# A recurrent-memory transformer with a planned instruction order: 64-column values in place while one layer runs, and seven early groups staged over the GpSimd DMA queue

## The chip, the cores and the metric

The kernel runs on one core of one Trainium2 chip. The metric is device time in microseconds (us), from the first to the last instruction of one execution. Before the change it is 1634.84 us, the median of three runs from 1634.42 to 1636.5 us. In the profile PE is TensorE (PEld is its weight load), DVE is VectorE, ACT is ScalarE, POOL is GpSimd and SP is SyncE. DMAs are issued from SP, ACT and POOL.

## The reference, cut to what matters

Two layers, each an attention over segments and a dense block, are applied to x of 2048 x 512. The attention is recurrent: 8 memory rows that come out of segment s go into segment s + 1.

```python
for s in range(n_seg):                       # 64 segments of 32 rows
    h = concat([mem, xs])                    # 8 + 32 = 40 rows
    q, k, v = h @ Wq, h @ Wk, h @ Wv         # 32 heads of 128
    p = softmax(where(mask, q @ k.T * scale, -1e9))
    o = (p @ v) @ Wo
    mem = o[:8]; outs.append(o[8:])
# x = x + A(layernorm(x));  x = x + relu(layernorm(x) @ w1) @ w2;  and both once more
```

## The kernel before, in words

**Steps.** The kernel walks through 68 steps. In step k, layer 0 works on segment k and layer 1 on segment k - 4 (`DELTA = 4`). So steps 0 to 3 have layer 0 alone with 40 columns, steps 4 to 63 have both layers side by side in 80 columns, and steps 64 to 67 have layer 1 alone. A step projects queries and keys for 32 heads (L1074), scores (L1103), runs the softmax on DVE and ACT (L1114 to L1145), turns the probabilities (L646), multiplies them with the values (L1187) and projects with Wo (L1214). The new memory columns are copied from PSUM into the next step's input tile `HT` by DVE (L1230). That copy ends one step and starts the next. After every second step a "dense unit" (`finish_pair`, `dense_layer`) does the dense block of two segments; its hidden tile is `hT`.

**Values.** The value rows of x do not depend on the recurrence. They are computed ahead by groups of four segments. Groups 0 to 5 (`EARLY = 5`) are *early*: `prepare_group` loads the rows, `layernorm` normalises and turns them, and `early_values` computes four 64-column units of eight matmuls each (L973) while the weights are still arriving. Groups 6 to 15 are *late*: pairs of groups are made in the steps by `late_values` (L944), eight units of four 128-column matmuls per pair. All late values and those of groups 1 to 5 are written to HBM (`vh`) and come back by DMA into the value tile `V0` as needed. Only the columns that hold the rest of a segment and its memory rows are computed in the step, with 32 columns (`values_narrow`, L992) in steps 1 to 3 and with 64 columns from step 4; they get from the tile `vw` into `V0` by DMA (L1026). Step 0 computes 40 columns straight into `V0` (`values_direct`, L1038). Group 0's rows wait in the tile `vg` (L1014).

**Where early data waits.** The rows of x land in two halves of `vw`. The values of groups 1 to 5 wait in the room of the weights `w1` and `w2` until POOL's queue has written them to HBM (L932). Their normalised rows wait in tiles `xg`. SP writes those to HBM (`xh`, L811) once the marker "loaded" says that step 1's values have been placed. The dense weights are loaded after that.

**Weights.** Wv (in three parts), Wq, Wk and Wo (in halves) are loaded at the start. All but the first part go over POOL's queue, and their order there is Wv, Wv, Wq, Wk, Wq, Wk, Wo, Wo (L498, L495).

**Order.** Every operation is put into a plan with a cost, what it reads and what it writes. `Plan.order` lists them by planned start, with priorities from the tables `PLACE` and `AHEAD` and four numbers in `RULE`. The program is written in that order, and each engine executes its instructions strictly in it. A DMA is modelled by `bulk` as an issue on the engine and a landing on a serial queue. The plan charges a matmul order that changes the column tiling (`tile`) with `TURN`.

A layernorm crosses four engines: DVE (L684, L687), POOL for the power of -1/2 (L690, L691), DVE for the scaling (L694), PE for the turn (L646), then ACT or DVE for the copy (L894, L896).

Of the kernel before, what the change touches and what calls it, by code (L numbers as in the profile page):

```python
# [26 lines left out]
WHOLE, COL64, EITHER, COL32 = range(4)  # L27
TURN = 0.096

RULE = (0.0731, 331.4491, 505.4188, 866559925356557.625)  # L30
PERIOD = 46.2777
PLACE = {
    ("attend.mmu0.0", 0): -152.667, ("attend.mmu0.0", 1): -118.912, ("attend.mmu0.0", 2): -639.225,
    ("attend.mmu0.0", 3): 328.193, ("attend.mmu0.0", 4): -173.499, ("attend.mmu0.0", 5): 386.967,
    ("attend.mmu0.0", 6): 449.133, ("attend.mmu1.0", 0): -183.38, ("attend.mmu1.0", 1): 433.744,
    ("attend.mmu1.0", 2): 361.711, ("attend.mmu1.0", 3): 441.403, ("attend.mmu1.0", 4): -122.568,
    ("attend.mmu1.0", 5): 199.077, ("attend.mmu1.0", 6): 581.404, ("attend.mmu2.0", 0): -862.741,
    ("attend.mmu2.0", 1): -762.821, ("attend.mmu2.0", 2): -99.412, ("attend.mmu2.0", 3): -218.396,
    ("attend.mmu2.0", 4): -720.778, ("attend.mmu2.0", 5): -60.014, ("attend.mmu2.0", 6): -142.579,
    ("attend.mmu3.0", 0): -166.299, ("attend.mmu3.0", 1): -129.893, ("attend.mmu3.0", 2): -1226.967,  # L40
    ("attend.mmu3.0", 3): 67.821, ("attend.mmu3.0", 4): -136.693, ("attend.mmu3.0", 5): -20.817,
    ("attend.mmu3.0", 6): 293.466, ("attend.mmu4.0", 0): 65.898, ("attend.mmu4.0", 1): -215.881,
    ("attend.mmu4.0", 2): 381.601, ("attend.mmu4.0", 3): 412.604, ("attend.mmu4.0", 4): -130.21,
    ("attend.mmu4.0", 5): -853.627, ("attend.mmu4.0", 6): 948.075, ("dense_layer.mm.0", 1): 732.94,
    ("dense_layer.mm.0", 3): 740.199, ("dense_layer.mm.0", 6): 839.326, ("dense_layer.mm.1", 1): -969.556,
    ("dense_layer.mm.1", 3): -286.677, ("dense_layer.mm.1", 6): 67.604, ("dense_layer.mm.2", 1): 398.19,
    ("dense_layer.mm.2", 3): 243.499, ("dense_layer.mm.2", 6): 419.477, ("dense_layer.mm.3", 1): 627.889,
    ("dense_layer.mm.3", 3): 181.496, ("dense_layer.mm.3", 6): 643.035, ("dense_layer.mm.4", 1): 161.37,
    ("dense_layer.mm.4", 3): 390.622, ("dense_layer.mm.4", 6): 400.054, ("dense_layer.mm.5", 1): 594.567,
    ("dense_layer.mm.5", 3): 753.248, ("dense_layer.mm.5", 6): 345.325, ("finish_pair.turn.0", 1): -144.39,  # L50
    ("finish_pair.turn.0", 3): -761.751, ("finish_pair.turn.0", 6): -878.802, ("g0", 2): -907.97,
    ("g1", 2): 259.128, ("g2", 2): -170.342, ("g3", 2): -266.685, ("g4", 2): -99.976, ("g5", 2): 565.774,
    ("late_values.mmv0.0", 0): 283.731, ("late_values.mmv1.0", 0): -248.92, ("late_values.mmv2.0", 0): -1018.714,
    ("late_values.mmv3.0", 0): 469.169, ("late_values.mmv4.0", 0): -1001.105, ("late_values.mmv5.0", 0): 1.489,
    ("late_values.mmv6.0", 0): -868.467, ("late_values.mmv7.0", 0): 433.155, ("layernorm.turn.0", 1): 337.759,
    ("layernorm.turn.0", 3): 441.922, ("layernorm.turn.0", 6): -292.588, ("layernorm.turn.1", 1): -863.663,
    ("layernorm.turn.1", 3): -167.818, ("layernorm.turnr.0", 0): -153.966, ("layernorm.turnr.0", 4): 426.349,
    ("layernorm.turnr.1", 0): 374.651, ("layernorm.turnr.1", 4): 594.017, ("prepare.turns.0", 2): -916.093,
    ("project.mm.0", 0): 352.884, ("project.mm.0", 1): 403.52, ("project.mm.0", 2): 426.265,
    ("project.mm.0", 3): 475.549, ("project.mm.0", 4): -8.363, ("project.mm.0", 5): 481.308,  # L60
    ("project.mm.0", 6): 364.213, ("project.mm.1", 0): 360.97, ("project.mm.1", 1): 250.905,
    ("project.mm.1", 2): 395.025, ("project.mm.1", 3): 90.611, ("project.mm.1", 4): -154.497,
    ("project.mm.1", 5): 342.487, ("project.mm.1", 6): -140.762, ("project.mm.2", 0): 69.475,
    ("project.mm.2", 1): 427.61, ("project.mm.2", 2): -910.526, ("project.mm.2", 3): 539.171,
    ("project.mm.2", 4): -962.774, ("project.mm.2", 5): 327.765, ("project.mm.2", 6): 570.292,
    ("project.mm.3", 0): 234.432, ("project.mm.3", 1): 212.581, ("project.mm.3", 2): 219.168,
    ("project.mm.3", 3): 1057.658, ("project.mm.3", 4): 374.948, ("project.mm.3", 5): 458.206,
    ("project.mm.3", 6): 1049.752, ("project.mm.4", 0): -906.842, ("project.mm.4", 1): -226.675,
    ("project.mm.4", 2): -119.077, ("project.mm.4", 3): 366.414, ("project.mm.4", 4): -955.316,
    ("project.mm.4", 5): 408.222, ("project.mm.4", 6): -222.974, ("queries_keys.mmu0.0", 0): -319.479,  # L70
    ("queries_keys.mmu0.0", 1): -311.142, ("queries_keys.mmu0.0", 2): -195.441,
    ("queries_keys.mmu0.0", 3): -783.942, ("queries_keys.mmu0.0", 4): -856.389,
    ("queries_keys.mmu0.0", 5): -1226.512, ("queries_keys.mmu0.0", 6): -189.749,
    ("queries_keys.mmu0.1", 0): -126.555, ("queries_keys.mmu0.1", 1): -875.245,
    ("queries_keys.mmu0.1", 2): -230.758, ("queries_keys.mmu0.1", 3): -218.806, ("queries_keys.mmu0.1", 4): -924.83,
    ("queries_keys.mmu0.1", 5): -998.214, ("queries_keys.mmu0.1", 6): -798.535, ("queries_keys.mmu0.2", 0): 1.933,
    ("queries_keys.mmu0.2", 1): -915.221, ("queries_keys.mmu0.2", 2): -763.206,
    ("queries_keys.mmu0.2", 3): -815.004, ("queries_keys.mmu0.2", 4): -155.478,
    ("queries_keys.mmu0.2", 5): -920.249, ("queries_keys.mmu0.2", 6): -766.935, ("queries_keys.mmu0.3", 0): -285.59,
    ("queries_keys.mmu0.3", 1): -134.747, ("queries_keys.mmu0.3", 2): 7.492, ("queries_keys.mmu0.3", 3): -23.601,  # L80
    ("queries_keys.mmu0.3", 4): -292.473, ("queries_keys.mmu0.3", 5): -193.042,
    ("queries_keys.mmu0.3", 6): -173.541, ("queries_keys.mmu1.0", 0): -40.306,
    ("queries_keys.mmu1.0", 1): -1010.704, ("queries_keys.mmu1.0", 2): -94.937,
    ("queries_keys.mmu1.0", 3): -233.672, ("queries_keys.mmu1.0", 4): -212.713,
    ("queries_keys.mmu1.0", 5): -961.418, ("queries_keys.mmu1.0", 6): -321.925,
    ("queries_keys.mmu1.1", 0): -965.925, ("queries_keys.mmu1.1", 1): -223.66, ("queries_keys.mmu1.1", 2): -323.504,
    ("queries_keys.mmu1.1", 3): 20.112, ("queries_keys.mmu1.1", 4): -146.653, ("queries_keys.mmu1.1", 5): -223.193,
    ("queries_keys.mmu1.1", 6): -158.937, ("queries_keys.mmu1.2", 0): -823.694,
    ("queries_keys.mmu1.2", 1): -932.252, ("queries_keys.mmu1.2", 2): -231.6, ("queries_keys.mmu1.2", 3): -250.634,
    ("queries_keys.mmu1.2", 4): 237.43, ("queries_keys.mmu1.2", 5): -250.953, ("queries_keys.mmu1.2", 6): -993.941,  # L90
    ("queries_keys.mmu1.3", 0): -189.715, ("queries_keys.mmu1.3", 1): -231.672,
    ("queries_keys.mmu1.3", 2): -257.674, ("queries_keys.mmu1.3", 3): -300.812,
    ("queries_keys.mmu1.3", 4): -145.268, ("queries_keys.mmu1.3", 5): -37.546, ("queries_keys.mmu1.3", 6): -183.014,
    ("queries_keys.mmu2.0", 0): 140.663, ("queries_keys.mmu2.0", 1): -210.356, ("queries_keys.mmu2.0", 2): -294.536,
    ("queries_keys.mmu2.0", 3): -112.732, ("queries_keys.mmu2.0", 4): 320.259, ("queries_keys.mmu2.0", 5): 215.543,
    ("queries_keys.mmu2.0", 6): -122.288, ("queries_keys.mmu2.1", 0): 428.309, ("queries_keys.mmu2.1", 1): 92.511,
    ("queries_keys.mmu2.1", 2): -899.997, ("queries_keys.mmu2.1", 3): 229.222, ("queries_keys.mmu2.1", 4): 280.866,
    ("queries_keys.mmu2.1", 5): 161.233, ("queries_keys.mmu2.1", 6): 27.508, ("queries_keys.mmu2.2", 0): 204.746,
# [82 lines left out]
    ("values_direct.ev", 1): -11.513, ("values_narrow.ev", 1): -7.969,  # L181
}

LOAD = {("v", 0): 4.4, ("v", 1): 3.8, "o": 2.95}
REST, SLOW = 2.75, 6.0

EARLY, SPREAD = 5, (0, 0, 2, 4, 4, 6, 8, 8)


def t_mm(n):  # L190
    return max(0.025, 0.0025 + n / 2400)


# [211 lines left out]
def kernel(  # L405
# [242 lines left out]
    class Early:  # L648

        def __init__(self, g):  # L650
            self.first, self.key = g % 2 == 1, ("xn", g)
            if self.first:
                hold[0] = p_x.buf()
# [698 lines left out]
```

## Time and profile before

| what | value |
|---|---|
| median of three runs | 1634.84 us |
| span of the profile | 1632.0 us |
| busy: PE, DVE, ACT, POOL | 97%, 68%, 64%, 9% |
| ends of steps 0, 1, 2, 3 (start of L1230, from the span's start) | 52.65, 70.62, 89.86, 106.84 us |
| late value matmuls (L944), by the program | 160 |
| 32-column value matmuls (L992) | 96 |
| early 64-column value matmuls (L973 on `xg` and `xnA`) | 160 + 32 |

A line of the timeline gives the start, the time, the engine, the line of the kernel, the operation, the tiles and, in brackets, the idle time of the engine before it with the work that ended it. In the slices, a digit is the busy share of a fortieth of the span in tenths.

### The profile page before, as it was taken

What the parts mean: (1) busy time and instruction counts of PE and PEld (TensorE: products, weight loads), DVE (VectorE), ACT (ScalarE), POOL (GpSimd) and SP (SyncE); (2) the same over time, 40 slices, a digit from 0 to 9 for tenths busy, and PEclk for the clock granted to TensorE, in tenths of its full rate; (3) what the DMA queues carried; (4) which work ended last, traced back from release to release, by engine and by line L of the source; (5) the groups of instructions that cost most, each with busy time, mean ns of one, the idle gap of its engine ahead of it and who ended that gap; (6) DMA issues with size and microseconds to landing.
All of it is one profiled execution on the core that took longest, in us unless ns stands there. A gap on an engine that the chain in (4) does not pass through costs nothing.

```text
span 1632.0 us, 88442 instructions
## 1 busy us (share of the span) xinstructions
PE 1589.6 (97%) x39898; PEld 1377.3 (84%) x39992; DVE 1111.6 (68%) x3091; ACT 1052.5 (64%) x2655; POOL 140.1 (9%) x352
## 2 busy tenths in 40 slices
PE   7999999999999999999999999999999999999997
PEld 4788888888888888888888888888888888888886
DVE  4566776776676676677667667667667767766765
ACT  5566666676666666666667666666666666666664
POOL 3100000000000100000100000100000000000000
PEclk9999999999999999999999999999999999999999
DMA  9720101110110110110110111110110100000000
GB/s 369 231 51 21 27 22 27 41 28 22 28 24 22 41 26 22 25 34 19 38 29 22 28 25 28 35 28 20 28 28 22 26 21 22 19 18 18 18 6 6
DMA packets 47097, 63.89 MB, mean 39 GB/s; under 512 B 17784, under 2 KB 33440, under 8 KB 46720
## 3 DMA queue, kind: packets, MB, share of 16 engines
q1 hardware_dynamic: 41136, 39.09, 10.0%
q0 software_dynamic: 4704, 18.35, 2.9%
q8 instruction: 313, 5.13, 1.4%
q10 hardware_dynamic: 880, 0.80, 0.2%
q14 instruction: 64, 0.52, 0.1%
HBM read 33.50 MB, written 11.93 MB: 28 GB/s over the span
## 4 chain that ended last, share of the span: by engine, by line
PE 92%; DMA 3%; DVE 2%; ACT 2%; issue 1%; POOL 0%; ACTq 0%; SPq 0%; POOLq 0%; DVEq 0%
PE work L1074 37%; PE st L1214 18%; PE fill L973 14%; PE fill L646 10%; PE work L1187 4%; PE work L1103 4%; DMA Wo_sb<-in_A_Wo_dram 2%; PE work L646 2%; PE fill L944 2%; ACT OT L894 1%; DVE HT L1230 0%; PE fill L992 0%; DMA vw<-in_A_x_dram 0%; ACT es L1125 0%; ACT PT L1168 0%
## 5 line engine op out<-in xcount | busy, mean ns | idle before, releaser
L1074 PE MATMUL work<-HT,Wk_sb 128*128 128x80 bf16 (+1 forms) x8704 | 355.7, 199 | 9.6 <-DVE HT L1230 8.8
L1074 PE MATMUL work<-HT,Wq_sb 128*128 128x80 bf16 (+1 forms) x8704 | 349.3, 199 | 1.3 <-DVE HT L1230 0.9
L1214 PE MATMUL st<-OT,Wo_sb 128*128 128x80 bf16 (+1 forms) x8704 | 344.5, 199 | 4.5 <-ACT OT L894 2.5
L1214 PEld LDWEIGHTS <-Wo_sb 128*128 128x128 bf16 x8704 | 324.9, 99 | 28.0 <-issue 5.2
L1074 PEld LDWEIGHTS <-Wq_sb 128*128 128x128 bf16 x8704 | 320.4, 99 | 26.4 <-issue 15.1
L1074 PEld LDWEIGHTS <-Wk_sb 128*128 128x128 bf16 x8704 | 321.6, 99 | 16.4 <-DVE HT L1230 13.3
L894 ACT CAST qT<-work 128x320 bf16<-128x320 f32 (+1 forms) x534 | 219.5, 412 | 76.8 <-PE work L1074 32.4
L973 PE MATMUL fill<-Wv_sb,HT 128*64 128x512 bf16 x2048 | 265.9, 381 | 0.0
L894 ACT CAST kT<-work 128x320 bf16<-128x320 f32 (+1 forms) x510 | 209.9, 412 | 82.5 <-PE work L1074 49.1
L894 ACT CAST OT<-work 128x320 bf16<-128x320 f32 (+1 forms) x404 | 158.1, 417 | 119.8 <-PE work L1187 117.3
L1168 ACT ACTIVATE PT<-work,half 128x320 bf16<-128x320 f32 (+2 forms) x384 | 170.9, 468 | 67.1 <-PE work L646 47.0
L894 ACT CAST vw<-fill 128x512 bf16<-128x512 f32 x203 | 119.0, 586 | 92.5 <-PE fill L973 82.0
L1114 DVE TENSOR_TENSOR es<-work,maskb 128x320 f32<-128x320 f32 (+2 forms) x340 | 136.8, 404 | 45.2 <-PE work L1103 40.3
L1170 DVE TENSOR_SCALAR PT<-work,half 128x160 bf16<-128x160 f32 (+2 forms) x296 | 127.5, 454 | 25.1 <-PE work L646 23.4
L973 PEld LDWEIGHTS <-HT 128*64 128x64 bf16 x2048 | 99.0, 110 | 52.1
L1125 ACT ACTIVATE es<-es 128x320 f32<-128x320 f32 (+2 forms) x340 | 137.6, 410 | 6.0 <-DVE es L1121 5.0
L1121 DVE TENSOR_TENSOR es<-es,mx 128x320 f32<-128x320 f32 (+2 forms) x340 | 136.7, 405 | 5.5
L1118 DVE TENSOR_REDUCE mx<-es 128x8 f32<-128x320 f32 (+2 forms) x340 | 135.2, 400 | 6.2
L1145 DVE TENSOR_TENSOR P<-es,sm 128x320 bf16<-128x320 f32 (+2 forms) x340 | 133.1, 408 | 5.3
L1230 DVE CAST HT<-st 128x64 bf16<-128x64 f32 (+1 forms) x67 | 14.8, 221 | 175.2 <-PE st L1214 175.2
L1128 DVE TENSOR_REDUCE sm<-es 128x8 f32<-128x320 f32 (+2 forms) x340 | 131.6, 396 | 2.5 <-ACT es L1125 1.6
L1103 PEld LDWEIGHTS <-qT 128*40 128x40 bf16 x4096 | 90.8, 98 | 44.8 <-ACT kT L894 10.2
(98 smaller groups left out, 1779.3 us busy)
## 6 DMA issues: line engine op xcount, KB each, us to landing
V<-vw SPq DMA_DIRECT2D x252, 48.0 KB
V<-vh SPq DMA_DIRECT2D x120, 64.0 KB
vh<-vg SPq DMA_DIRECT2D x40, 128.0 KB
Wq_sb<-in_A_Wq_dram POOLq DMA_DIRECT2D x2, 2048.0 KB, 21.3
Wk_sb<-in_A_Wk_dram POOLq DMA_DIRECT2D x2, 2048.0 KB, 25.8
Wo_sb<-in_A_Wo_dram POOLq DMA_DIRECT2D x2, 2048.0 KB, 36.7
Wv_sb<-in_A_Wv_dram POOLq DMA_DIRECT2D x1, 2048.0 KB, 11.8
vh<-w_sb POOLq DMA_DIRECT2D x4, 512.0 KB, 9.9
```

The source lines that it names most:

```text
L646: nc.tensor.matmul(out_[u:v, :], lhsT=lhsT[:, u:v], rhs=rhs, start=start, stop=stop, tile_position=(0, u))
L894: nc.scalar.copy(out=out_, in_=in_)
L973: nc.tensor.matmul(vp[64 * b:64 * b + 64, :], lhsT=cols(c4), rhs=Wv_sb[:, c4, n * 512:(n + 1) * 512], start=(c4 == 0), stop=(c4 == NC4 - 1 ...
L1074: nc.tensor.matmul(qp[:, hi * 2 * L:hi * 2 * L + n], lhsT=W_sb[:, c4, h * Dh:(h + 1) * Dh], rhs=HT[:, c4, c0:c1], start=(c4 == 0), stop=(c ...
L1103: nc.tensor.matmul(v[64 * g2:64 * g2 + L, a, i, b, :], lhsT=qT[:, hi, a * L:(a + 1) * L], rhs=kT[:, hi, a * L:(a + 1) * L], start=True, st ...
L1114: nc.vector.tensor_tensor(out=flat(es[:, A]), in0=flat(sp[:, A]), op=ALU.add, in1=maskb[:, a_lo:a_hi, :].unsqueeze(2).to_broadcast([128, n ...
L1118: nc.vector.tensor_reduce(out=mx[:, As], in_=es3(), axis=AX.X, op=ALU.max)
L1121: nc.vector.tensor_tensor(out=es3(), in0=es3(), op=ALU.subtract, in1=mx[:, As].unsqueeze(2).to_broadcast([128, ns * na, L]))
L1125: nc.scalar.activation(out=es[:, A], in_=es[:, A], func=ACTF.Exp, scale=SCALE)
L1145: (nc.gpsimd if eng == POOL else nc.vector).tensor_tensor(out=o, in0=flat(es[:, A]), op=ALU.mult, in1=sm[:, As].rearrange("p (a s) -> p a ...
L1168: nc.scalar.activation(out=o, in_=i, func=ACTF.Copy, scale=half[:, b:b + 1])
L1214: nc.tensor.matmul(wo[:, 2 * W * c4 + c0:2 * W * c4 + c1], lhsT=Wo_sb[:, h, c4 * 128:(c4 + 1) * 128], rhs=OT[:, h, c0:c1], start=(h == 0 a ...
```

## The change

The change does five things.

1. *One layer only: 64 columns in place.* In steps 0 to 3, `values` computes columns 0 to 63 of `HT` (the 32 rows of the segment, the memory and columns of the other layer) and evicts them whole into `V0`. `values_direct`, `values_narrow` and the column tiling by 32 are gone, and with them the DMAs that place values in steps 1 to 3 and group 0's early values in `vg`.
2. *Seven early groups.* `EARLY` is 7. Groups 6 and 7 are computed with the other early groups, and their values wait in `vg` and `vw`, which nothing else needs yet.
3. *Rows in dense-unit tiles.* The rows of x of the early groups land in two parts of `hT`. Group 7's normalised rows wait in an `OX` tile.
4. *Staging over POOL.* The normalised rows of early groups go to HBM over POOL's DMA queue (`bulk(POOL, ...)`) as soon as they exist, no longer over SP after the marker "loaded".
5. *A new plan.* Late groups start at step 6 and every 12 steps, spread by (0, 0, 2, 4, 4, 6, 8, 10). `RULE`, `PERIOD`, `PLACE` and `AHEAD` have new numbers, so the order changes everywhere.

```diff
-WHOLE, COL64, EITHER, COL32 = range(4)
+WHOLE, COL64, EITHER = range(3)
-EARLY, SPREAD = 5, (0, 0, 2, 4, 4, 6, 8, 8)
+EARLY, SPREAD = 7, (0, 0, 2, 4, 4, 6, 8, 10)
...
-    p_xv = Pool([vw[:, 2 + i, :] for i in range(2)], True)
+    p_xv = Pool([p_h.tiles[0][:, 4 * i:4 * i + 4, :].rearrange("p f t -> p (f t)") for i in range(2)], True)
...
+        if g > 5:
+            return (vg, vw)[g - 6][:, p0:p0 + n, :]
...
-                hold[0] = p_x.buf()
+                hold[0] = (p_x if g < 7 else p_ox).buf()
...
+        if early:
+            def put():
+                nc.gpsimd.dma_start(out=out_, in_=halves_of(xnT))
+
+            bulk(POOL, 0.78, put, ("xh", g), 0.125, w=[("xh", g)], uses=on(xnT))
+            early_values(g, xnT)
...
     def step_values(k):
-        if k == 0:
-            values_direct(HTs[0][:, :, 0:L], deps)
-            return
-        if 1 in act:
-            values(lambda c4: HTs[i][:, c4, HS:2 * L], lambda p: vw[:, p, :], ("vw",), deps)
+        if k < DELTA:
+            values(lambda c4: HTs[i][:, c4, 0:64], lambda p: V0[:, p, :], lambda p: [("V0", p, b) for b in range(2)], deps)
         else:
-            values_narrow(HTs[i][:, :, HS:HS + 32], deps)
-        place_values(k, False)
+            values(lambda c4: HTs[i][:, c4, HS:2 * L], lambda p: vw[:, p, :], lambda p: [("vw", p)], deps)
+            place_values(k, False)
...
-    start = {g: DELTA + 10 * i for i, g in enumerate(pairs)}
+    start = {g: DELTA + 2 + 12 * i for i, g in enumerate(pairs)}
...
-        if k == 1:
-            for put in later:
-                put("loaded")
```

## Prediction

> **What bounds the kernel now.** I read the page's slices first, then the chain of waits, then the timeline of the start by engine.
>
> ```profile
> PE 1589.6 (97%) x39898; PEld 1377.3 (84%) x39992; DVE 1111.6 (68%) x3091; ACT 1052.5 (64%) x2655; POOL 140.1 (9%) x352
> ...
> PE   7999999999999999999999999999999999999997
> PEclk9999999999999999999999999999999999999999
> DMA  9720101110110110110110111110110100000000
> ```
>
> PE is full in all slices but the first and last, and the DMA engines are full only in the first. So there are two stages: a start that ends when the weights have landed, and then a stream of PE work. The chain in order of time shows the seam:
>
> ```profile
> 11.99 38.80 DMA Wo_sb<-in_A_Wo_dram
> 50.83 1.80 PE st L1214 x64
> 54.15 3.07 PE fill L992 x28
> ```
>
> The second half of Wo lands at 11.99 + 38.80 = 50.79 us; then only 64 matmuls of step 0 are left, and step 0 ends at 52.65 (L1230). What else PE does until 50.8 is nearly free; what is queued behind 50.8 is paid in full. The landings follow from the views by line: Wq 21.8, Wk 28.2, Wq 33.6, Wk 38.7 and Wo 45.0 us. POOL in the same stretch:
>
> ```profile
> 28.55 0.22 POOL L690 TENSOR_SCALAR ln<-ln 128x1 f32<-128x1 f32 x1 [6.13 <-DVE ln L687]
> 28.85 0.57 POOL L691 TENSOR_TENSOR ln<-ln,mhalf 128x1 f32<-128x1 f32 x1
> ...
> 43.09 1.20 POOL L932 DMA_DIRECT2D vh<-w_sb  x2 [13.66 <-ACT es L1125]
> 44.46 0.29 POOL L913 COPY HT<-xnA 128x128 bf16<-128x128 bf16 x1 [0.17 <-PE work L1074]
> 44.70 1.06 POOL L932 DMA_DIRECT2D vh<-w_sb  x2
> ```
>
> All layernorm powers of early groups (L690, L691) are done by 29.4, *before* the first staging DMA. That DMA then holds POOL idle for 13.66 us, and nobody needs POOL meanwhile.
>
> ```profile
> DMA to landing us min/median/max: 8.6/9.8/10.9
> ```
>
> This is the view of line L932. Put in at 43.1, behind Wo in the same queue, the first staged values land at 52.1, just after Wo's 50.8: the queue keeps its order.
>
> **What the Trainium skill says.** "DMA: Bandwidth & Descriptors", section "Anatomy of one DMA", says that DMA engines do not wait on semaphores; a wait is held by the issuing sequencer before dispatch. The 13.66 us of idle POOL agree. The same page, "Two DMAs through the same engine are not ordered", says that descriptors of one queue start in order; the landing at 52.1 behind 50.8 agrees. "TensorE: Matmul & The Clock Gate", Part 1, says that an idle window of about 3.4 us halves PE's clock until a busy one has passed; the granted clock is 0.50 between 54 and 56 us, after the wait for Wo, and 28 matmuls of L992 take 3.07 us there, against 16 in about 1.05 elsewhere.
>
> **The change, part by part.**
>
> *Staging over POOL.* The order of the changed program tells the decisive thing. POOL's DMAs use eight completion semaphores in turn, and each issue first waits for the DMA eight places earlier. The eight weight loads take the first turn. Then POOL's program goes on, each item strictly after the one before: rows of group 1 (waits for Wv), powers of groups 2 and 3, values of group 1 and rows of group 2 (wait for Wv and Wq), power of group 4, values of 2 and rows of 3 (wait for Wk and the second Wq, 33.6), power of group 5, values of 3 and rows of 4 (wait for the second Wk, and for the *first half of Wo*, 45.0), power of group 6, values of 4 and rows of 5 (wait for the *second half of Wo*, 50.8, and for group 1's rows, which lie behind it), power of group 7. Before, there were no powers behind such waits.
>
> Queued behind these powers: DVE's scaling of that group stands in DVE's order ahead of the softmax of step 0, and PE's turn of group 6 stands ahead of the second halves of Wq and Wk, that of group 7 ahead of the last keys and of eight value units. So PE stops three times.
> - Group 5: power after 33.6, so its turn is at about 35.5, while PE has run out at about 30. PE then has 6 to 7 us of values; this stop is only partly paid.
> - Group 6: 45.0 + issue 0.55 + power 0.87 (28.55 to 29.42) + scaling 0.41 + 0.1 = 47.0. Then 96 projections of 40 columns, 2.5 us at 25 ns each (64 of L1074 take 1.67 us of weight loads), and PE is empty at about 50.
> - Group 7: one more load of 128 KB beside the weights delays Wo by 0.3, so 51.1 + two issues at 0.55 + 0.87 + 0.41 + 0.1 = 53.6.
>
> Behind group 7's turn still stand, all on PE: the turn 0.4, 32 projections 0.8, the wait for its copy 0.4, eight value units (four of group 7, four of group 6) at 0.866 (eight matmuls of L973) 6.9, scores, turns, attends and changes of tiling about 1.5, and all 128 matmuls of Wo 3.4 (64 took 1.80 with their end). That is 13.4. The idle time before it halves the clock for some 3 us (+1.3). Step 0 ends at 53.6 + 13.4 + 1.3 = 68.3 instead of 52.65: **+15.6 us**. I bound it by 12.5 (no slow clock, waits inside filled) and 18.
>
> *64 columns in place.* A step's values were 32 matmuls of 32 columns, four abreast, 2 x 0.866 = 1.73; they become four units, 3.46: +5.2 over steps 1 to 3. Two units of early groups are left over for step 1: +1.7. Late values and turns of the first late pair leave steps 2 and 3: -2.1. The slow clock of step 1 has moved: -1.4. The placing DMAs (3.7 us of issues on SP after `vw` is ready, but PE waited only 0.4 us for V) give -0.5. Sum **+2.9** (+1 to +5). Group 0's early values (-3.46) are in step 0's sum.
>
> *Fewer late values.* 160 matmuls of L944 become 128. Their price is read from step lengths, from one L1230 to the next in DVE's timeline:
>
> ```profile
> 153.86 0.23 DVE L1230 CAST HT<-st 128x64 bf16<-128x64 f32 x1 [2.18 <-PE st L1214]
> 179.22 0.23 DVE L1230 CAST HT<-st 128x64 bf16<-128x64 f32 x1 [3.31 <-PE st L1214]
> 202.24 0.22 DVE L1230 CAST HT<-st 128x64 bf16<-128x64 f32 x1 [2.73 <-PE st L1214]
> 227.60 0.23 DVE L1230 CAST HT<-st 128x64 bf16<-128x64 f32 x1 [3.30 <-PE st L1214]
> ```
>
> These are steps 6, 7 and 8: 25.36, 23.02 and 25.36 us. An odd step without late values is 22.09 us (1336.77 to 1358.85), with one unit 22.47 (227.60 to 250.07), with two 23.01, for part of a unit fills PE's waits for the softmax. Before: 14 steps of two, 10 of one, from step 4 on, 14 x 0.92 + 10 x 0.38 = 16.7; after, by the program's order: 8 and 16, 13.4. So -3.3, and not the full 8 units x 0.866 = -6.9. One late pair fewer to normalise: -0.3.
>
> *The new order of the 60 double steps.* Step by step PE has the same work and as many changes of tiling (4 and 6 in even and odd steps). More dense matmuls go in 64-column halves (in the timeline 32 halves take 1.02 us, 64 ns a pair, and 16 whole ones 0.90, 56 each), which the steps with that form before show as at most 0.1 us: +1.4. The turns of groups 8 and 9 fall into step 4: +0.5. Waits of DVE and ACT inside a step can move by 0.15 us a pair either way, +-5 us in all. Sum with the late values: **-1.7**.
>
> *At nothing:* the tiles of `hT` and `OX` are free until the first dense unit in step 2, 20 us after; the dense weights wait for staged values that land near 60 us and are first used in step 2; `vg` and `vw` are needed from step 4. PE's work of steps 1 and 2 hides all of it.
>
> Sum: 1634.8 + 15.6 + 2.9 - 1.7 = 1651.6 us.
>
> **The rivals.**
> - *The start is hidden* (6%). If the waits of POOL's issues were met early, groups 6 and 7 would fill PE's idle time before 50.8 (3.7 us from 10 us on), step 0 would end at about 54, and the late values would come off. 1634.8 + 1.3 + 2.9 - 6.9 = 1632 us. It is what the change is for. Against it speaks that each wait stands ahead of a power on the same engine, and that landings are bound by DMA at 400 GB/s.
> - *The same with the saving small* (4%): 1634.8 + 1.3 + 2.9 - 1.7 - 2 = 1635 us.
> - *The start costs, but the stream gains* (20%). If late values save their whole 6.9 and the new order loses a little less in waits, 1634.8 + 13 + 1 - 6.9 = 1642.
> - *Start and stream both lose* (20%). Slow clock twice, and 0.2 us in each of 30 pairs: 1651.6 + 2 + 6 = 1660.
>
> **How the numbers follow.** The likeliest, at 50%, is the stall with an unchanged stream, 1651.6. The range reaches to the 1642 and 1660 cases. Faster 0.06, same 0.04, slower 0.90.
>
> **What would show it.** Right: POOL lines of the new row DMAs with idle time just before 45 to 46 and 51 to 52 us, ended by the weights' DMA; L695 at about 45.6 and 52.2; PE idle 3 to 5 us before the turns that follow; the first memory copy (L1182) near 68 us, the next three about 19, 20 and 18 us apart; then pairs of steps near 48 us. Wrong: the first copy near 54, which would mean that POOL never waited for Wo; or pairs of steps that differ by more than 0.2 us from before, which would put the cause into the stream.

## The result, and the profile after

The kernel after the change takes 1645.74 us (median of four runs, 1644.46 to 1647.37), against 1634.88 before (the three runs above and a fourth); the ratio is 1.0065, with a 95% interval of 1.0048 to 1.0083. It is slower, as forecast, by 10.9 us instead of 16.8. The two profiled executions differ by more, 1645.7 against 1632.0 us: that of after is the slowest of its four runs, that of before is 0.7 us faster than the fastest of its four. So the parts below add up to 13.7, and they are those of single executions.

The page of the kernel after, the lines that answer to those shown of before:

```profile
PE 1600.5 (97%) x40154; PEld 1374.4 (84%) x40154; DVE 1097.8 (67%) x3096; ACT 1056.8 (64%) x2622; POOL 158.0 (10%) x387
...
PE   6899999999999999999999999999999999999998
...
PEclk9899999999999999999999999999999999999999
DMA  9521101101110110111011111101111000000000
```

What is new stands in the first slices: PE is less full in the first two, its clock is lower in the second, and the DMA engines have less to do there. The memory copies that end the steps (DVE's timeline of after) give the sizes:

```profile
67.38 0.19 DVE L1182 CAST HT<-st 128x32 bf16<-128x32 f32 x1 [3.40 <-PE st L1166]
84.39 0.19 DVE L1182 CAST HT<-st 128x32 bf16<-128x32 f32 x1 [1.35 <-PE st L1166]
107.37 0.19 DVE L1182 CAST HT<-st 128x32 bf16<-128x32 f32 x1 [2.09 <-PE st L1166]
123.31 0.19 DVE L1182 CAST HT<-st 128x32 bf16<-128x32 f32 x1 [0.48 <-PE st L1166]
```

| part | before | after | difference | forecast |
|---|---|---|---|---|
| step 0 ends at | 52.65 | 67.38 | +14.7 | +15.6 |
| steps 1, 2, 3 | 17.97, 19.24, 16.98 | 17.02, 22.98, 15.94 | +1.7 | +2.9 |
| steps 4 to 66 | 1495.45 | 1492.99 | -2.5 | -1.7 |
| from there to the end | 29.7 | 29.4 | -0.3 | 0 |

POOL's timeline of after shows the forecast chain, to within half a us:

```profile
33.58 0.55 POOL L817 DMA_DIRECT2D xh<-xg  x1 [4.87 <-DMA Wq_sb<-in_A_Wq_dram]
34.15 0.24 POOL L695 TENSOR_SCALAR ln<-ln 128x1 f32<-128x1 f32 x1
...
45.41 0.55 POOL L817 DMA_DIRECT2D xh<-xg  x1 [5.78 <-DMA Wo_sb<-in_A_Wo_dram]
45.99 0.24 POOL L695 TENSOR_SCALAR ln<-ln 128x1 f32<-128x1 f32 x1
...
51.42 0.62 POOL L937 DMA_DIRECT2D vh<-w_sb  x1 [4.54 <-ACT kT L900]
52.04 0.55 POOL L817 DMA_DIRECT2D xh<-xg  x1
52.61 0.24 POOL L695 TENSOR_SCALAR ln<-ln 128x1 f32<-128x1 f32 x1
```

The three L695 shown are the powers of groups 5, 6 and 7. Each has no idle time of its own (no bracket): it starts the moment the DMA issue before it is through, and that issue waited. At 51.42 the profile names ACT's copy of `kT`, which this DMA does not read; the second half of Wo landed at 50.89, as long before as the first half before 45.41 (44.88). PE's timeline shows what hangs on them:

```profile
35.55 0.61 PE L649 MATMUL fill<-ident,xr 128*128 128x128 bf16 x4 [4.30 <-DVE xr L699]
...
47.67 0.48 PE L1139 MATMUL work<-PT,V 128*64 128x80 bf16 x8 [3.04 <-DVE PT L1122]
47.89 0.69 PE L649 MATMUL fill<-ident,xr 128*64 128x128 bf16 x8
...
54.01 0.61 PE L649 MATMUL fill<-ident,xr 128*128 128x128 bf16 x4 [2.12 <-DVE xr L699]
...
90.99 0.41 PE L1026 MATMUL work<-HT,Wk_sb 128*128 128x40 bf16 x8 [2.73 <-issue]
```

Group 5's turn comes at 35.55 (forecast 35.5). The stop at 47.67 is the softmax, which stands on DVE behind the scaling that waits for group 6's power. The last line is something that I had not forecast: in step 2 PE stops 2.73 us in the middle of a group of 16 equal matmuls, ended by nothing that the profile knows ("issue").

### The profile page after: what moved, and what is told of

It reads as the page before. It is cut to its first block, busy times and chain, and to the rows that moved or that the text cites. A ratio compares the mean times of both kernels' runs of the same rounds, so it can differ in the third digit from the quotient of the medians.

```text
span 1645.7 us, 88944 instructions
## 1 busy us (share of the span) xinstructions
PE 1600.5 (97%) x40154; PEld 1374.4 (84%) x40154; DVE 1097.8 (67%) x3096; ACT 1056.8 (64%) x2622; POOL 158.0 (10%) x387
## 3 DMA queue, kind: packets, MB, share of 16 engines
q8 instruction: 314, 5.14, 1.3%
## 4 chain that ended last, share of the span: by engine, by line
PE 89%; ACT 2%; DVE 1%; issue 0%; DMA 0%; POOLq 0%; SPq 0%; DVEq 0%; POOL 0%; ACTq 0%
PE work L1026 35%; PE st L1166 18%; PE fill L973 13%; PE fill L649 10%; PE work L1139 4%; PE work L1055 4%; PE work L649 2%; PE fill L949 2%; ACT OT L900 1%; DVE HT L1182 0%; ACT PT L1120 0%; ACT es L1077 0%; PE fill L771 0%; DMA V<-vw 0%; ACT vw L900 0%
## 5 line engine op out<-in xcount | busy, mean ns | idle before, releaser
L1026 PE MATMUL work<-HT,Wq_sb 128*128 128x80 bf16 (+1 forms) x8704 | 368.2, 200 | 9.9 <-DVE HT L1182 9.5
L973 PE MATMUL fill<-Wv_sb,HT 128*64 128x512 bf16 x2176 | 274.1, 384 | 0.0
L900 ACT CAST qT<-work 128x320 bf16<-128x320 f32 (+1 forms) x485 | 198.0, 409 | 109.0 <-PE work L1026 75.0
L900 ACT CAST kT<-work 128x320 bf16<-128x320 f32 (+1 forms) x540 | 221.6, 410 | 70.1 <-PE work L1026 17.9
L1120 ACT ACTIVATE PT<-work,half 128x160 bf16<-128x160 f32 (+1 forms) x418 | 181.5, 464 | 53.2 <-PE work L649 31.6
L900 ACT CAST OT<-work 128x320 bf16<-128x320 f32 (+1 forms) x358 | 143.7, 415 | 82.6 <-PE work L1139 81.9
L900 ACT CAST vw<-fill 128x512 bf16<-128x512 f32 x174 | 101.8, 585 | 80.2 <-PE fill L973 72.1
L1080 DVE TENSOR_REDUCE sm<-es 128x8 f32<-128x320 f32 (+2 forms) x340 | 128.7, 394 | 15.6 <-ACT es L1077 15.4
L1122 DVE TENSOR_SCALAR PT<-work,half 128x320 bf16<-128x320 f32 (+2 forms) x262 | 116.9, 456 | 18.9 <-PE work L649 17.1
L1097 DVE TENSOR_TENSOR P<-es,sm 128x320 bf16<-128x320 f32 (+2 forms) x313 | 123.3, 411 | 2.6
L1055 PEld LDWEIGHTS <-qT 128*40 128x40 bf16 x4096 | 81.2, 98 | 40.6 <-ACT kT L900 10.2
```

The source lines that it names most:

```text
L900: nc.scalar.copy(out=out_, in_=in_)
L973: nc.tensor.matmul(vp[64 * b:64 * b + 64, :], lhsT=cols(c4), rhs=Wv_sb[:, c4, n * 512:(n + 1) * 512], start=(c4 == 0), stop=(c4 == NC4 - 1 ...
L1026: nc.tensor.matmul(qp[:, hi * 2 * L:hi * 2 * L + n], lhsT=W_sb[:, c4, h * Dh:(h + 1) * Dh], rhs=HT[:, c4, c0:c1], start=(c4 == 0), stop=(c ...
L1055: nc.tensor.matmul(v[64 * g2:64 * g2 + L, a, i, b, :], lhsT=qT[:, hi, a * L:(a + 1) * L], rhs=kT[:, hi, a * L:(a + 1) * L], start=True, st ...
L1080: nc.vector.tensor_reduce(out=sm[:, As], in_=es3(), axis=AX.X, op=ALU.add)
L1120: nc.scalar.activation(out=o, in_=i, func=ACTF.Copy, scale=half[:, b:b + 1])
```

## The experiments

The first four kernels change the order in which the program of after is written out, and only POOL's order moves by it; PE, DVE, ACT and SP have the same sequence as after the change. The last two, with added bursts, were run once each, for their traces.

**All staging behind the last power.**

```diff
-        for o in plan.order():
+        ops = plan.order()
+        stage = ("*prepare_group.put", "*early_values.put")
+        power = {o.group: i for i, o in enumerate(ops) if o.kind == "*layernorm.power"}
+        last = power["7"]
+        behind = [o for o in ops[:last] if o.kind in stage]
+        ops = [o for o in ops[:last + 1] if o not in behind] + behind + ops[last + 1:]
+        for o in ops:
```

> My theory (POOL's powers of groups 5, 6 and 7 are held by the staging DMAs in front of them): with all staging DMAs issued behind group 7's power, PE's order unchanged, L695 of groups 5, 6, 7 runs before 38 us, PE no longer stops for the turns of groups 6 and 7, and step 0 ends at 53 to 56 us instead of 67.4. Total 1645.7 - 12.5 = about 1633 us (1630 to 1636). The stop in step 2 stays. Rival (PE has too much early work, or the rows of x come too late): step 0 ends after 63 us and the total stays above 1641.

It took 1634.05 us (ratio to before 1.0000, 0.9992 to 1.0008), and step 0 ends at 54.10. POOL's timeline of this kernel:

```profile
34.00 0.28 POOL L695 TENSOR_SCALAR ln<-ln 128x1 f32<-128x1 f32 x1 [6.11 <-DVE ln L692]
...
37.42 0.22 POOL L695 TENSOR_SCALAR ln<-ln 128x1 f32<-128x1 f32 x1 [2.49 <-DVE ln L692]
...
45.35 0.54 POOL L817 DMA_DIRECT2D xh<-xg  x1 [3.79 <-DMA Wo_sb<-in_A_Wo_dram]
51.36 0.54 POOL L937 DMA_DIRECT2D vh<-w_sb  x1 [5.46 <-DMA Wo_sb<-in_A_Wo_dram]
```

The last two powers now wait for their own statistics (DVE L692) and are done by 38.3. The issues still wait for both halves of Wo, until the same times, but nothing that PE needs is behind them. The rival falls: with the same PE order the two more groups fit into the time before Wo. The change's loss in the start, 13.3 of 14.7 us, is the place of the powers on POOL.

**Only the staging between the powers of groups 6 and 7.**

```diff
-        behind = [o for o in ops[:last] if o.kind in stage]
+        behind = [o for o in ops[power["6"]:last] if o.kind in stage]
```

> Only the staging DMAs between the powers of groups 6 and 7 go behind the power of 7. My theory: group 6's power still waits for the first half of Wo (L695 at 46), group 7's follows at about 47 instead of 52.6, the second stop is gone, and step 0 ends at 47.0 + 0.4 + 2.5 + 13.0 = about 63 us (62 to 65). Total about 1641.5 us (1639 to 1644). Rival (the second stop costs nothing, for Wo's second half binds anyway): step 0 ends at 67 and the total stays at 1645.

1640.83 us (1.0043, 1.0028 to 1.0058); step 0 ends at 63.64. Group 6's power is still at 45.82, group 7's comes at 48.35 after its own statistics, and PE's stop ahead of group 7's turn (2.12 us after the change) is gone. So of the stops, with the slow clock after them, the last one is worth 3.7 us and those for groups 5 and 6 the other 9.5.

**Staging of groups 6 and 7 later.** The stop in step 2 falls into a stretch in which the DMA engines are full: POOL's four DMAs issued from 82.36 to 83.95 and the second load of dense weights on SP's queue (from 82.88).

```diff
+        put = [o for o in ops if o.kind in stage and o.group in "67"]
+        ops = [o for o in ops if o not in put]
+        at = min(i for i, o in enumerate(ops) if o.kind == "finish_pair.widen" and o.step == 3)
+        ops = ops[:at] + put + ops[at:]
```

> Staging of groups 6 and 7 (four DMAs, 0.77 MB, at 82 to 84 us after the change) goes behind the second dense load, ahead of the residual copies of step 3, near 103 us; all else as after the change. Theory (PE's stop of 2.7 us in step 2 comes from its instruction fetch, held back by these DMAs and the dense weights together): no stop ended by issue over 1 us in step 2, step 2 takes 20 to 21 us instead of 23.0, total about 1643 us (1641 to 1645). Rival (the stop is PE's own, or the dense weights alone make it): a stop of 2 to 3 us near 90 us stays and the total is 1645 to 1646.

1644.21 us (1.0057, 1.0042 to 1.0072). The total alone can't tell 1.5 us from nothing, but the trace can. First the kernel after, then this one, the same view of the stretches by engine; the row is step 2 (time, PE busy, ..., clock, DMA share, GB/s):

```profile
84.49:107.47 22.98, 20.09 (x571) 16.37 (x573) 11.64 (x47) 11.30 (x38) 2.43 (x5) 0.93 0.39 128
```

```profile
85.16:104.17 19.01, 18.54 (x571) 15.87 (x573) 11.64 (x47) 11.18 (x38) 4.62 (x9) 1.00 0.39 135
```

The same 571 matmuls in 19.01 instead of 22.98 us: the stop shrank from 2.73 to 0.32 us, and the half clock that followed it (91.1 to 94.5 us after the change) is gone. Part came back in step 3, which takes 16.72 instead of 15.94, with a stop of 0.43. The dense weights are still loaded in this stretch, so alone they leave 0.32 us of the stop. What stopped PE can be seen in the queues. In the view of the DMA queues from 80 to 88.5 us, after the change:

```profile
DMA packets 1041, 1.72 MB, mean 202 GB/s; under 512 B 82, under 2 KB 802, under 8 KB 1041
...
q1 hardware_dynamic: 751, 0.74, 34.9%
q0 software_dynamic: 290, 0.98, 29.5%
```

and in the same stretch with the staging moved:

```profile
q1 hardware_dynamic: 1298, 1.28, 46.8%
q0 software_dynamic: 80, 0.26, 8.2%
q8 instruction: 2, 0.03, 1.8%
```

The "instruction" queue q8 carries 314 packets of 16 KB in the whole kernel, 5.14 MB, which is 64 bytes for each of PE's 80,300 matmuls and weight loads. Normally one starts about every 4 us in these steps. In the busy stretch after the change none does between 79.6 and 88.6 us, and PE stops at 88.3.

That packet has been moved at 89.56, and PE goes on at 90.99. The traces of all ten kernels agree. Between 20 and 1600 us they have 23 stops of 0.25 us or more that end by "issue", and 22 of them end 1.25 to 1.61 us after an instruction packet has been moved. In the kernels with the PE order of after, the 13 such stops up to step 2 also stand whole multiples of 256 of PE's loads and matmuls apart, the content of a packet. So in these stops PE waits for its instructions.

**Both edits.**

> Both edits together: all staging behind group 7's power, and that of groups 6 and 7 moved on to step 3. Theory: the gains add, step 0 ends at 53 to 56 us, step 2 takes 20 to 21 us, total about 1630.5 us (1628 to 1634), faster than before the change by 0.1 to 0.4%. Rival (the gain of the start is lost again in steps 1 to 3): ends of step 3 at 112 us or later, total 1634 us or more.

1632.35 us (0.9982, 0.9975 to 0.9989): faster than before the change, by 0.11 to 0.25%. Steps 0 to 3 end at 54.34, 73.59, 92.50 and 108.78. This is the version to keep. In the profiled executions its start is still 1.9 us behind the kernel before at the end of step 3, and it gains 4.1 us in steps 4 to 66 (1491.31 against 1495.45).

**Rows over SP again.** The reason for POOL's wait could be the number of DMAs ahead or a full queue. Undoing one part of the change tells the two apart.

```diff
             def put():
-                nc.gpsimd.dma_start(out=out_, in_=halves_of(xnT))
+                nc.sync.dma_start(out=out_, in_=halves_of(xnT))
```

> One part of the change undone: the normalised rows of early groups go to HBM over SP again (L817), at the same places of the program; PE's order stays as after the change. Theory (each POOL issue waits for the DMA eight places earlier, so what counts is how many POOL DMAs stand ahead of a power): with only the values on POOL, the one ahead of group 6's power waits for the first Wk (27.8) and not for Wo, and the one ahead of group 7's for Wq's second half (33.3); step 0 ends at 53 to 57 us and the total is 1632 to 1636 us. Rows sent over SP's own queue now share the DMA engines with the weights (0.66 MB, up to 1.6 us on Wo). Rival (POOL is held because its queue is full of weights, whatever the count): group 6's power stays near 45 us and step 0 ends after 63.

1634.35 us (0.9993, 0.9985 to 1.0002); step 0 ends at 56.46. POOL's timeline of this kernel:

```profile
34.60 0.28 POOL L695 TENSOR_SCALAR ln<-ln 128x1 f32<-128x1 f32 x1 [5.41 <-DVE ln L692]
...
35.49 0.62 POOL L937 DMA_DIRECT2D vh<-w_sb  x1
38.22 0.22 POOL L695 TENSOR_SCALAR ln<-ln 128x1 f32<-128x1 f32 x1 [2.11 <-DVE ln L692]
...
39.05 0.63 POOL L937 DMA_DIRECT2D vh<-w_sb  x1
```

These are the powers of groups 6 and 7 and the fourth and fifth DMA behind the eight weight loads. Neither of them waits, although three weight loads are still under way in the queue (they land at 41.04, 47.12 and 52.98). In the kernel after, the sixth DMA behind the weights went out at 39.02, the seventh at 45.41 and the eighth at 51.42, each 0.5 us after the sixth, seventh and eighth weight load had landed (38.49, 44.88, 50.89). So it is the count of eight, not a full queue. The price of SP shows too: rows sent while the weights arrive push Wo's second half from 50.89 to 52.98.

**64 columns in place, alone.** In the kernel before:

```diff
     def step_values(k):
...
-        if k == 0:
-            values_direct(HTs[0][:, :, 0:L], deps)
-            return
+        if k < DELTA:
+            values_in_place(k, lambda c4: HTs[i][:, c4, 0:64], deps)
+            return
```

> The kernel before with one part of the change alone: in steps 0 to 3 the values are 64 columns computed into V0, and the placing DMAs of these steps and group 0's early values are gone; five early groups, rows over SP, numbers of the plan as before. The plan orders the program anew with them. Theory of the prediction (the extra units are paid): steps 1 to 3 take 54.2 + 5.2 - 0.5 - 1.4 = 57.5 us, step 0 ends at 50 to 53, total 1636 to 1640. Rival (in steps 1 to 3 PE idles 3.5 us in the kernel before, in part for values on their way by DMA, and the extra units go there): steps 1 to 3 take 54 to 55.5 us, total 1632 to 1636.

The rest of the edit takes out the placing DMAs of these steps and group 0's early values, and gives one choice of the planner a default. 1636.95 us (1.0010, 1.0001 to 1.0019). Step 0 ends at 53.37, just outside its range, and steps 1 to 3 take 57.19 us instead of 54.19. The rows of the view of stretches that sum the three steps, of the kernel before and of this one:

```profile
sum 54.19, PE 50.71 PEld 42.95 DVE 33.12 ACT 32.88 POOL 6.60; mean PE 16.90 PEld 14.32 DVE 11.04 ACT 10.96 POOL 2.20
```

```profile
sum 57.19, PE 53.55 PEld 44.62 DVE 34.56 ACT 35.91 POOL 6.56; mean PE 17.85 PEld 14.87 DVE 11.52 ACT 11.97 POOL 2.19
```

PE is idle 3.5 us before and 3.6 us here. The extra units do not go into idle time; they are paid, and the rival falls. How much they cost is less sure than 3.0 us: in the two burst runs below, which are the kernel before up to step 25, steps 1 to 3 took 55.37 and 55.30 us, and the medians of the totals differ by 1.4 us. So 1.8 to 3.0 us is what these executions show.

**Bursts added.** Transfers that nobody needs, in the kernel before, to see whether they alone stop PE.

```diff
+        extra = {26: 2, 36: 4, 46: 8}
+        spare = [dram.tile([128, 4, 512], BF, name=f"spare{i}") for i in range(14)]
         for o in plan.order():
+            if o.kind == "prep_x.cp" and o.step in extra:
+                for i in range(extra.pop(o.step)):
+                    nc.gpsimd.dma_start(out=spare.pop()[:], in_=vh[1 + i % 3][:])
```

> The kernel before with transfers that nobody waits for, HBM to HBM on POOL's queue: 1, 2 and 4 MB in steps 26, 36 and 46, all else the same. Theory (PE's instructions come by DMA and a burst holds them back): PE stops in the middle of a group, ended by issue: not at 1 MB, 0 to 2 us at 2 MB, 3 us or more at 4 MB, and no instruction packet starts for over 8 us there. Rival (such stops have another cause): no stop ended by issue in these steps; a step is longer only where PE waits for values V whose DMA comes late.

The 1 MB burst costs nothing, the 2 MB one makes a step of 24.55 us out of 22.46, the 4 MB one 30.56 out of 22.46. But this run shows nothing of the instructions. The 2 MB step waits 1.9 us for values by name ("DMA V<-vw"). The stop of 6.04 us in the 4 MB step is put down to "issue", but stands just ahead of L1187, which reads V, whose DMAs were in the same burst. It is the one of the 23 that does not fit: it ends 3.8 us after an instruction packet had been moved. So it was most likely V. What it does show is that V's placing DMAs are delayed by a burst on another queue.

**Bursts behind V.** The same with the burst reading V itself, so that it starts when V has been placed.

```diff
+            if o.kind == "project.mm" and o.step in extra:
+                for i in range(extra.pop(o.step)):
+                    nc.gpsimd.dma_start(out=spare.pop()[:], in_=V0[:])
```

> As the run with added bursts, but each burst starts only when the value tile V has been placed, and reads V, so that nothing PE needs in that step comes by DMA behind it: 2, 3 and 4 MB on POOL's queue in steps 53, 57 and 61 of the kernel before (22.09 us each there). Theory (PE's instructions come by DMA): the bursts take 5, 8 and 10.5 us at 400 GB/s; the step with 4 MB has a stop of 1 to 5 us ended by issue and a gap of over 8 us between two instruction packets, that with 2 MB none. Rival (the stop of 6.0 us in the run before was a wait for V alone): no stop ended by issue at any size, steps within 0.3 us of 22.09 apart from waits with a name, such as those for the layernorm whose power stands behind the issues on POOL (up to 4 us).

PE's timeline of this kernel has two stops of "issue" in the three stretches:

```profile
1413.82 0.83 PE L973 MATMUL fill<-Wv_sb,HT 128*64 128x512 bf16 x5 [0.86 <-issue]
...
1507.81 0.78 PE L1074 MATMUL work<-HT,Wq_sb 128*128 128x80 bf16 x17 [0.91 <-issue]
```

Each stands in the middle of a group of equal matmuls (after the third of eight, after the fifteenth of 32), where there is nothing to wait for, and ends 1.5 us after an instruction packet had been moved. With 2 MB (full from 1309 to 1316) instruction packets start at 1310.6 and 1314.7, and there is no stop. With 3 MB none starts between 1402.2 and 1411.4, with 4 MB none between 1497.3 and 1505.4. The steps in which these bursts fall, 58 and 62, take 26.62 and 26.45 instead of 25.36 us. From 130 to 1600 us no trace without added bursts has such a stop. So a burst that no instruction waits for does stop PE; the stop is smaller than I expected, 0.9 us and not 1 to 5, and the 3 MB burst did as much as the 4 MB one. Perhaps it counts when the burst meets the next fetch, and not its length alone; that was not varied.

## Why the prediction was right, and where it was not

**The start.** Right in mechanism and size. The turn of group 6 came at 47.89 (forecast 47.0), that of group 7 at 54.01 (53.6), the end at 67.38 (68.3). The work behind group 7's turn was the mis-sized term: 67.38 - 54.01 = 13.4 us with the clock at half until 56.97, so with 1.5 us of slow clock in it, against a forecast of 13.4 plus 1.3. The small work and the waits were put too high. From the first value unit to Wo PE took 8.25 us (55.62 to 63.87), some 7.6 without the slow clock, against 8.4 (6.9 + 1.5), and the wait of 0.4 us for the turn's copy did not come. The prediction cites an idle window of about 3.4 us as what halves the clock. The traces do not show a whole idle window: PE had been busy 2.09 of the 3.42 us ahead of the half clock in the kernel before (49.79 to 53.21), and 0.68 of 3.41 us in step 2 of after. That the wait is a count of eight was read from the order of the program; the runs with POOL's order changed and with rows over SP show it.

**Steps 1 to 3.** The sum, +1.7 against +2.9, is near by luck, for two errors of opposite sign: forecast were steps of about 19, 20 and 18 us, measured 17.0, 23.0 and 15.9. The extra 64-column units alone make 57.19 out of 54.19, +3.0, where the forecast has +3.3 for this part of the change, but 1.8 against the other executions of the same start. The new order, though, fills PE's waits of these steps better: with the staging later and the stop all but removed, the same steps take 17.02 + 19.01 + 16.72 = 52.74, 1.5 us *less* than before and 4.4 less than forecast, and PE is idle for 1.1 us of them. I had worked the units out as PE work and left the 3.5 us of idle time in the kernel before standing. With both edits they take 54.44, since the fetch now stops PE in step 1. On the other side, the step "At nothing" failed: it said that PE's work of steps 1 and 2 hides the staged values and the dense weights. PE needed none of these data, but it needed the DMA engines for its own instructions, and stopped 2.73 us, with half clock after it. Together with the slow clock that is 55.93 - 52.74 = 3.2 us that my working did not hold.

**The stream.** Forecast -1.7, measured -2.5; in the other five runs with this PE order -3.0 to -4.2. The odd steps from 5 to 63 carry what is regular in it: 679.38 us before, 677.00 after, -2.4. After, steps of no, one and two late units take 22.10, 22.49 and 23.04 us, where before had 22.09, 22.47 and 23.01, and there are 8 steps of two and 16 of one, as counted: -3.3 was the right term, less some 0.03 a step. The rival that late units save their whole 6.9 us falls: a unit of 0.87 us is worth 0.4 to 0.5. The terms for dense halves (+1.4) and for the turns in step 4 (+0.5) did not show: the usual even step takes 25.32 against 25.36, and step 4 24.47 against 24.54. The rest is in a few even steps of 25.8 to 26.2 us, which differ from run to run.

**The rivals.** "The start is hidden" gave 1632 us if POOL's waits were met early. They were not, but once the powers stand ahead of them the kernel takes 1634.05, and with the burst moved as well 1632.35. So the change does hold a gain: the total is that of the rival, though in the profile the start gives 1.9 us away and the stream gains 4.1; the place of six instructions on POOL turned it into a loss.

What stays open: the runs do not say why an instruction packet comes late while the other queues are busy, only that it does.

## What to carry to other kernels

A DMA issue is not free of waits: on POOL here it waits for the DMA eight places before it, so count the DMAs in front of any small operation on the issuing engine that others need, and put that operation first. When data are staged "for nothing", ask what else shares the DMA engines; PE's own instructions do, and bursts stopped it here in the middle of a matmul group for up to 2.7 us. A total that comes out near the forecast is not yet a working that is right: here an unseen gain of some 4 us and an unseen stop of some 3 nearly cancelled.

## What the runs showed of the hardware that I had not expected

PE's instructions come by DMA, in packets of 16 KB for 256 instructions, one about every 4 us in the one-layer steps. "Runtime: NRT & Kernel Launch" of the Trainium skill, section "Instruction fetch mechanics", says the same of the blocks and that the fetch is mostly hidden. From 130 to 1600 us that holds in all kernels without added bursts. In step 2 of the kernels with one PE order a longest gap between packets of 6.4 us came with a stop of 0.3 us at most (staging later, both edits), two gaps of 5.9 and 5.8 us in a row with 1.1 us (rows over SP), and gaps of 8.4, 8.4 and 9.0 us with 2.1, 2.2 and 2.7 us. The kernel before has such a stop too, of 0.80 us at the end of step 2. Where the DMA engines are full for longer, the fetch falls behind step by step: in the kernel with both edits packets start at 38.3, 45.1, 51.4, 56.6 and 61.5 us, and PE has four stops of 0.7 to 1.1 us between 40 and 64. The section gives PE room for 2048 instructions, which is eight packets, though a note in it speaks of two lines of 16 KiB. The runs bear out two: in step 2 PE is empty 8.4 to 8.7 us after the last packet started, two packets' worth at one in 4 us.
